# Three hand-ordered steps and 64 bytes of memory in a fused recurrence, expert and MLP kernel

## The chip, the core and the metric

The kernel runs on one core of a Trainium2 chip. The metric is the time of one execution in microseconds of the device. The engines are TensorE (PE, with its weight loads as PEld), VectorE (DVE), ScalarE (ACT), GpSimd (POOL) and SyncE (SP); SP, ACT and POOL issue transfers (SPq, ACTq, POOLq in the rows).

## The reference

Three stages follow one another. A gated linear recurrence over 768 tokens for 4 batches of 8 heads with 48 dimensions; a layer of 8 experts, in which each of the 3072 tokens goes to the expert with the largest logit; an MLP with a squared rectifier.

```
for t in range(S):                                   # attention, S = 768, D = 48
    cur = einsum('bhd,bhe->bhde', u * k[t], v[t])
    y[t] = einsum('bhd,bhde->bhe', r[t], state + cur)
    state = w[t] * state + einsum('bhd,bhe->bhde', k[t], v[t])
logits = x @ w_gate; e_idx = argmax(logits)          # x: 3072 x 384, 8 experts
out[mask] = gate * sigmoid(x @ w_output_gate)[e] * (relu(x[mask] @ w1[e]) @ w2[e])   # F = 1024
h = relu(x @ w_in); y = (h * h) @ w_out              # d_ff = 2048
```

## The kernel before

**Recurrence.** The work is cut into 16 units (4 batches times 4 pairs of heads). `load` fetches one unit's `w`, `k`, `r` and `v` in rows of 48 floats (192 bytes) into the tiles `nat` (`wN`, `kN`, `rN`, `vN`), 2 or 3 buffers of each, 128 partitions by 12 rows; a row stands every 256 bytes. These tiles are the first of the pool `ac`, which lies behind the pool `cst` of constants and small tables; a tile's address follows from the sizes of those made ahead of it. `w_check` (ACT) squares a unit's `w` for a check of its range, two units ahead; `scores` (PE) is followed by ACT copies of its banks (L738), and the turns of `k` and `r` (`k_turn`, `r_turn`, L663) reuse these banks.

**Order.** In all stages the order of instructions on each engine is the order of the code (`manual_schedule`), and each engine takes its own in that order.

**Routing.** `route_steps` of a batch makes the logits from `xT` (matmuls at L169, one per pair of heads and third of the tokens), copies them as `lt` (ACT, L172), turns them (L177), picks the expert, ranks the tokens (L216, L217) and scatters the rows to `x_rows` (POOL, L246). It is a generator: `route_step` runs it up to its next `yield`. `finish_routing` then makes the order of the experts (`bei`) and a `flag`, behind which every engine branches ("rare": values that the fast path doesn't hold for).

**Experts.** A first block of 320 tokens of expert 0 (`blkA`) starts ahead of the end of the routing, from rows of the first three batches. Its rows are gathered (`xg`, POOL, L397), scaled (DVE, L408) and turned by `prep_x` (PE, L427; hi and lo halves by ACT and DVE). `up` and `down` are its steps, nine matmuls each (L341 to L343). Behind the branch come the blocks of the 8 experts in order of size; block 0 has 128 tokens. Its words `w1r`, `w2r` are fetched in two halves by `load` (SP, L321 and L322). `expert_of` reads a number of `bei` into a register of SP. Ahead of the first words of block 1 stands a transfer of four bytes into `spare`: SP waits there for the transfers that wrote its source.

**MLP.** `down2` adds up the second product for 512 tokens in four groups of 128. In its last call the groups take the last three pieces of the hidden dimension (13, 14 and 15) one after the other; a group's end is followed by an addition (DVE, L1183) and a scatter to the output (POOL, L1185).

Of the kernel before, what the change touches and what calls it, by code (L numbers as in the profile page):

```python
# [9 lines left out]
F32 = mybir.dt.float32  # L10
F32R = mybir.dt.float32r
BF16 = mybir.dt.bfloat16
I32 = mybir.dt.int32
# [8 lines left out]
def rwkv_moe_kernel(  # L22
# [15 lines left out]
    nc = tc.nc  # L38
    B, H, S, D = r.shape
    NT, DM = out.shape  # L40
    E, _, F = w1.shape
# [26 lines left out]
    x_rows = dram.tile([NT + 1, WR], F32, name="x_rows")  # L68
# [4 lines left out]
    cst = ctx.enter_context(tc.tile_pool(name="cst", bufs=1))  # L73
# [23 lines left out]
    bvals = cst.tile([128, E, Q], F32, name="bvals")  # L97
    bcom = cst.tile([128, E], F32, name="bcom")
    bei = cst.tile([1, E], I32, name="bei")
    spare = cst.tile([1, E], I32, name="spare")  # L100
    tail = cst.tile([128, B, NTB, 2], F32, name="tail")
    xoff = cst.tile([128, E], F32, name="xoff")
    xend = cst.tile([128, E], F32, name="xend")
# [201 lines left out]
    def block_rows():  # L305
        rows_of(gi, bvals, E, B - 1)
        nc.vector.tensor_copy(off, bcom[0:1])
# [31 lines left out]
    def three(out_, a, b, a_of, b_of, start, stop):  # L339
        (ah, al), (bh, bl) = a, b  # L340
        nc.tensor.matmul(out_, a_of(ah), b_of(bh), start=start, stop=False)  # L341
        nc.tensor.matmul(out_, a_of(ah), b_of(bl), start=False, stop=False)  # L342
        nc.tensor.matmul(out_, a_of(al), b_of(bh), start=False, stop=stop)  # L343
# [204 lines left out]
    def block_of(P, k, e):  # L548
        we = [t[e:e + 1] if isinstance(e, int) else t[ds(e, 1)] for t in (w1, w2)]
        return Block(P, CAPS[k], *we, lambda n, i: gi[:n, k, i:i + 1], (k + 1) % 2)  # L550
# [7 lines left out]
    def expert_of(k):  # L558
        return nc.values_load(bei[0:1, k:k + 1], engines=(ET.SP,), min_val=0, max_val=E - 1)
# [3 lines left out]
    P = Pools("m", True)  # L563
# [6 lines left out]
    def route_step():  # L570
        return next(routing[B - 1], 0)

    with ExitStack() as actx:
# [312 lines left out]

        blkA = first["A"]
        blkA.ps_w, blkA.w_names = ps_t, ["pt"] * KD
        blkA.prep_x(0)
        blkA.prep_x(1)  # L890
        route_step()
        route_step()
        units[-1].back()
        blkA.prep_x(2)
# [9 lines left out]
    def put_ids_A():  # L904
        own = []
        for i in range(blkA.nt):
            n = blkA.rows(i)
            ins = nc.sync.dma_start(x2_ids[ds(column(offA, i) if i else 0, n)], blkA.ids[:n, i:i + 1])
            for o in own:
                tc.declare_no_dep(ins.ins, o.ins, reason="columns of their own")  # L910
            own.append(ins)

    with tc.manual_schedule(engines={ET.PE, ET.DVE, ET.Activation, ET.SP, ET.Pool}):
        put_ids_A()
        blkA.prep_w(FA, nc.vector)
        route_step()
        route_step()
        blkA.up(0)
        route_step()
        route_step()  # L920
        route_step()
        blkA.up(1)
        nc.vector.tensor_scalar(flag[:, 0:1], pf[:1, :1], 0.0, None, op0=ALU.is_le)
        blkA.down(0)
        more = None
        while more is None:
            nc.gpsimd.memset(warm, 0.0)
            more = route_step()
        tc.mark_branch_hint_location("rare", "LikelyTaken", [ET.PE, ET.DVE, ET.SP])
        finish = finish_routing()  # L930
        next(finish)
        blkA.prep_w1(FA + 1, nc.vector)
        blkA.prep_w2(FA + 1, part="hi")
        for f in range(2, FA):
            blkA.up(f)
            if f == 2:
                next(finish)
                next(finish)
                blk1 = block_of(P, 1, expert_of(1))
                nc.sync.dma_start(spare[:, 0:1].bitcast(F32), x_rows[0:1, 0:1])  # L940
                blk1.load(0)
            blkA.down(f - 1)
        for _ in finish:
            pass
        blkA.down(FA - 1)
# [4 lines left out]
    with tc.If(rare > 0, label="rare"):  # L950
        fine = nc.values_load(flag[0:1, 0:1], min_val=0, max_val=1)
        with tc.If(fine == 0):
# [57 lines left out]
                    route(b, xT, xr, fk, ps_x, True)  # L1010
            for _ in finish_routing():
                pass
            blk1.words_of(expert_of(1))
            blk1.load(0, True)
            blkA.ps_w, blkA.w_names = ps_x, ["px"] * KD
            blkA.again(FA)
            put_ids_A()
# [49 lines left out]
    NI = GT // 128  # L1067
    NPRE = 3

    FH = KF2 // 2  # L1070
# [4 lines left out]
    wi, wo, rows, ids, w2raw, converted = {}, {}, {}, {}, {}, {}  # L1075
# [69 lines left out]
    xs, gs, pos, parts = {}, {}, {}, {}  # L1145
# [17 lines left out]
    def down2(s, f, last=False):  # L1163
        fs, l = divmod(f, FH)
        if l == 0:
            pos[s] = []
            for i in range(NI):
                slot = (KD + NI * s + i) % (2 * KD)
                pos[s].append((ps_o if slot < KD else ps_x).tile([128, 512], F32, name=f"po{slot}" if slot < KD else "px"))
        for i in range(NI):  # L1170
            for q in (f - 2, f - 1, f) if last else (f,):
                three(pos[s][i][:, :DM], gs[s, q], wo[q], lambda t: t[:, i * 128:(i + 1) * 128], lambda t: t, q % FH == 0, q % FH == FH - 1)
            if l == FH - 1:
                n = s % NG * NI + i
                ob = parts.pop(n) if fs else obp.tile([128, DM], F32, name="ob")
                if fs == 0:
                    if i % 2:
                        nc.vector.tensor_copy(ob, pos[s][i][:, :DM])
                    else:
                        nc.scalar.copy(ob, pos[s][i][:, :DM])  # L1180
                    nc.sync.dma_start(part[n], ob)
                    continue
                nc.vector.tensor_tensor(ob, pos[s][i][:, :DM], ob, op=ALU.add)  # L1183
                nc.gpsimd.memset(warm, 0.0)
                ins = nc.gpsimd.indirect_dma_start(out=out[:, :], out_offset=IndirectOffsetOnAxis(ap=tokc[:, n:n + 1], axis=0),  # L1185
                                                   in_=ob, in_offset=None)
                for o in stores:
                    tc.declare_no_dep(ins.ins, o.ins, reason="rows of their own")
                stores.append(ins)
# [16 lines left out]

    with tc.manual_schedule(engines={ET.PE, ET.DVE, ET.Activation, ET.SP, ET.Pool}):
        block_rows()
        blocks = [block_of(P, 0, 0), blk1]
        blk0 = blocks[0]  # L1210
        blk0.w1t, blk0.w2t = blkA.w1t, blkA.w2t
        blk0.gather()
        atA = [column(offA, i) if i else 0 for i in range(blkA.nt)]
        blk0.banks(1)
        for f in range(FA, KF):
            blkA.up(f)
            if f + 2 < KF:
                blkA.prep_w(f + 2, nc.vector)
            if f > FA:
                blkA.down(f - 1)  # L1220
            if f == FA:
                blkA.prep_w2(FA + 1, nc.vector, part="lo")
            if f == FA + 1:
                for k in range(1, E):
                    if k == 1:
                        blk1.words_of(expert_of(k))
                    else:
                        blocks.append(block_of(P, k, expert_of(k)))
                    blocks[k].banks((k + 1) % 2)
                blocks[1].load(1)  # L1230
                convert_load(0)
            if f == KF - 1:
                blk0.prep_x(0)
# [34 lines left out]
        for n in range(KF, E * KF):  # L1268
            e, f = divmod(n, KF)
# [65 lines left out]
        for n, (s, f) in enumerate(steps2):  # L1335
            l = f % FH
# [59 lines left out]
```

## Time and profile before

| | us |
|---|---|
| median of 3 runs | 832.16 (830.5 to 833.28) |
| the profiled execution | 830.97 |
| its span, first to last instruction | 829.1 |
| PE busy in the span | 799.8 (96%) |
| DVE busy | 531.0 (64%) |
| ACT busy | 374.5 (45%) |
| POOL busy | 352.5 (43%) |

The rows further below come from the profiled execution. Times are us from the start of its span; a line such as L341 is that of the kernel. PEclk is the share of full clock that TensorE was granted (1.00 is 2.4 GHz, 0.50 is 1.2 GHz). A DMA share over 1 means that packets overlap on the transfer engines. Matmuls are pipelined, so a busy PE is not one at its peak.

### The profile page before, as it was taken

What the parts mean: (1) busy time and instruction counts of PE and PEld (TensorE: products, weight loads), DVE (VectorE), ACT (ScalarE), POOL (GpSimd) and SP (SyncE); (2) the same over time, 40 slices, a digit from 0 to 9 for tenths busy, and PEclk for the clock granted to TensorE, in tenths of its full rate; (3) what the DMA queues carried; (4) which work ended last, traced back from release to release, by engine and by line L of the source; (5) the groups of instructions that cost most, each with busy time, mean ns of one, the idle gap of its engine ahead of it and who ended that gap; (6) DMA issues with size and microseconds to landing.
All of it is one profiled execution on the core that took longest, in us unless ns stands there. A gap on an engine that the chain in (4) does not pass through costs nothing.

```text
span 829.1 us, 15685 instructions
## 1 busy us (share of the span) xinstructions
PE 799.8 (96%) x5964; PEld 724.7 (87%) x5964; DVE 531.0 (64%) x958; ACT 374.5 (45%) x792; POOL 352.5 (43%) x433
## 2 busy tenths in 40 slices
PE   4999999899999999999999999999999999999995
PEld 4888888778889999999989998888899999999994
DVE  7888899865666777788444788888533434434342
ACT  4677666633454455545453433434333333333321
POOL 7675868722534545554751333324111313212122
PEclk9999999969999999999999999999999999999998
DMA  9998899315677667678651132231203203022011
GB/s 154 156 151 128 160 149 278 109 47 193 223 121 218 194 157 281 195 194 190 200 163 57 48 124 77 96 115 58 76 18 127 92 24 114 26 90 77 1 48 38
DMA packets 157365, 102.90 MB, mean 124 GB/s; under 512 B 112350, under 2 KB 140942, under 8 KB 157286
## 3 DMA queue, kind: packets, MB, share of 16 engines
q1 hardware_dynamic: 149046, 86.55, 42.4%
q0 software_dynamic: 4912, 14.65, 5.4%
q10 hardware_dynamic: 3328, 0.66, 0.6%
q8 instruction: 48, 0.79, 0.4%
q14 instruction: 31, 0.25, 0.1%
HBM read 79.34 MB, written 22.50 MB: 123 GB/s over the span
## 4 chain that ended last, share of the span: by engine, by line
PE 60%; issue 12%; POOL 4%; DVE 0%; POOLq 0%; ACT 0%; DVEq 0%; ACTq 0%
PE ph L342 10%; PE ph L341 10%; PE ph L343 10%; PE po L341 5%; PE po L343 5%; PE po L342 5%; PE px L343 5%; PE px L341 5%; PE px L342 5%; POOL out_dram L1185 2%; PE px L427 1%; PE po L427 0%; POOL x22l L336 0%; POOL x21l L336 0%; POOL x20l L336 0%
## 5 line engine op out<-in xcount | busy, mean ns | idle before, releaser
L1160 DVE SCALAR_TENSOR_TENSOR gg<-ph,rl 128x512 f32<-128x512 f32 x96 | 66.2, 689 | 120.9 <-ACT rl L1158 120.9
L1158 ACT ACTIVATE rl<-ph 128x512 f32<-128x512 f32 x96 | 57.5, 599 | 144.6 <-PE ph L343 144.5
L336 DVE TENSOR_TENSOR gl<-gg,gh 128x512 fp32r<-128x512 f32 x96 | 66.7, 695 | 65.9 <-ACT gh L334 41.2
L334 ACT CAST gh<-gg 128x512 fp32r<-128x512 f32 x96 | 59.6, 620 | 104.3 <-DVE gg L1160 104.3
L336 POOL TENSOR_TENSOR w1l<-w1r,w1h 128x384 fp32r<-128x384 f32 x56 | 59.6, 1070 | 66.8 <-ACT w1h L334 66.4
L330 ACT ACTIVATE hh<-ph 128x320 fp32r<-128x320 f32 (+7 forms) x64 | 32.5, 508 | 114.4 <-PE ph L343 111.7
L1106 POOL TENSOR_TENSOR caf<-caf,cbf 128x384 f32<-128x384 f32 x32 | 32.6, 1018 | 114.0 <-DVE cbf L1105 114.0
L336 DVE TENSOR_TENSOR w2l<-w2r,w2h 128x384 fp32r<-128x384 f32 x64 | 64.5, 1011 | 20.1 <-ACT w2h L334 19.5
L331 DVE SCALAR_TENSOR_TENSOR hl<-ph,hh 128x320 fp32r<-128x320 f32 (+7 forms) x64 | 36.9, 576 | 38.6 <-ACT hh L330 38.3
L1185 POOL DMA_INDIRECT out_dram<-ob,tokc x24 | 23.5, 977 | 67.2 <-DVE ob L1183 65.0
L341 PE MATMUL po<-hh,w2h 128*128 128x320 f32 (+4 forms) x120 | 42.8, 357 | 0.0
L342 PE MATMUL po<-hl,w2h 128*128 128x320 f32 (+4 forms) x120 | 41.8, 348 | 0.0
L343 PE MATMUL po<-hh,w2l 128*128 128x320 f32 (+4 forms) x120 | 41.6, 347 | 0.0
L336 POOL TENSOR_TENSOR x22l<-x2r,x22h 128x512 fp32r<-128x512 f32 x12 | 15.5, 1293 | 51.5 <-ACT x22h L334 51.5
L336 POOL TENSOR_TENSOR x21l<-x2r,x21h 128x512 fp32r<-128x512 f32 x12 | 15.5, 1295 | 45.4 <-ACT x21h L334 45.4
L397 POOL DMA_INDIRECT xg<-x_rows,gi x28 | 29.1, 1039 | 11.3 <-issue 5.4
L246 POOL DMA_INDIRECT x_rows<-xr,dsi x24 | 24.1, 1005 | 22.4 <-DVE dsi L232 16.4
L334 ACT CAST w2h<-w2r 128x384 fp32r<-128x384 f32 x64 | 32.9, 516 | 0.0
L334 ACT CAST w1h<-w1r 128x384 fp32r<-128x384 f32 x64 | 32.7, 512 | 0.0
L736 PE MATMUL pt<-rA,kT 64*128 64x128 f32 x306 | 31.4, 300 | 1.0 <-DVE rA L705 1.0
L336 POOL TENSOR_TENSOR x20l<-x2r,x20h 128x512 fp32r<-128x512 f32 x12 | 15.5, 1294 | 35.9 <-ACT x20h L334 35.9
L718 POOL TENSOR_TENSOR gv<-vN,g 128x576 f32<-128x576 f32 x16 | 18.5, 1154 | 28.7 <-PE pt L663 10.7
(859 smaller groups left out, 2651.7 us busy)
## 6 DMA issues: line engine op xcount, KB each, us to landing
w1r<-in_moe_w_dram SPq DMA_DIRECT2D x16, 768.0 KB, 7.4
w2r<-in_moe_w_dram SPq DMA_DIRECT2D x16, 768.0 KB, 7.4
x2r<-x_cols SPq DMA_DIRECT2D x12, 768.0 KB, 4.9
cq<-in_moe_w_in_dram SPq DMA_DIRECT2D x16, 384.0 KB, 4.7
cq<-in_moe_w_out_dram SPq DMA_DIRECT2D x16, 384.0 KB, 6.0
vN<-in_v_dram SPq DMA_DIRECT2D x32, 144.0 KB, 4.1
part<-ob SPq DMA_DIRECT2D x24, 192.0 KB, 2.0
ob<-part SPq DMA_DIRECT2D x24, 192.0 KB, 3.1
```

Of the source, the lines that this page charges most:

```text
L330: nc.scalar.activation(hi, src, AF.Relu)
L331: nc.vector.scalar_tensor_tensor(lo, src, 0.0, hi.bitcast(F32), op0=ALU.max, op1=ALU.subtract)
L334: nc.scalar.copy(hi, src)
L336: lo_eng.tensor_tensor(lo, src, hi.bitcast(F32), op=ALU.subtract)
L341: nc.tensor.matmul(out_, a_of(ah), b_of(bh), start=start, stop=False)
L342: nc.tensor.matmul(out_, a_of(ah), b_of(bl), start=False, stop=False)
L343: nc.tensor.matmul(out_, a_of(al), b_of(bh), start=False, stop=stop)
L736: nc.tensor.matmul(pa[j][:, ci], self.kT[pp, hf * HC + ci], self.rA[pp, hf * HC + ci], start=True, stop=True)
L1106: nc.gpsimd.tensor_tensor(af, af, bf, op=ALU.add)
L1158: nc.scalar.activation(rl, ph, AF.Relu)
L1160: nc.vector.scalar_tensor_tensor(gg, ph, 0.0, rl, op0=ALU.max, op1=ALU.mult)
L1185: ins = nc.gpsimd.indirect_dma_start(out=out[:, :], out_offset=IndirectOffsetOnAxis(ap=tokc[:, n:n + 1], axis=0), in_=ob, in_offset=None)
```

## The change

It has four parts. `spare` is 24 integers long in place of 8, which moves all tiles behind it on the left side of the memory by 64 bytes. The `route_step` that holds the last logits of the last batch stands ahead of `blkA.prep_x(0)` and `prep_x(1)`. The last call of `down2` goes through its groups and pieces in a list of its own. The first words of block 1 are fetched behind the branch, after all experts' numbers were read and the rows of block 0 have landed, where the four bytes now come from; the code that fetched them again in the rare branch falls away.

```diff
-    spare = cst.tile([1, E], I32, name="spare")
+    spare = cst.tile([1, 3 * E], I32, name="spare")
...
+        route_step()
         blkA.prep_x(0)
         blkA.prep_x(1)
-        route_step()
         route_step()
         units[-1].back()
         blkA.prep_x(2)
...
             if f == 2:
                 next(finish)
                 next(finish)
-                blk1 = block_of(P, 1, expert_of(1))
-                nc.sync.dma_start(spare[:, 0:1].bitcast(F32), x_rows[0:1, 0:1])
-                blk1.load(0)
             blkA.down(f - 1)
...
-        for i in range(NI):
-            for q in (f - 2, f - 1, f) if last else (f,):
-                three(pos[s][i][:, :DM], gs[s, q], wo[q], ...)
-            if l == FH - 1:
+        order = [(i, f) for i in range(NI)]
+        if last:
+            order = [(0, f - 2), (1, f - 2), (2, f - 2), (0, f - 1), (1, f - 1), (0, f), (1, f),
+                     (2, f - 1), (2, f)] + [(NI - 1, q) for q in (f - 2, f - 1, f)]
+        for i, q in order:
+            three(pos[s][i][:, :DM], gs[s, q], wo[q], ...)
+            if q % FH == FH - 1:
...
         blk0.gather()
         atA = [column(offA, i) if i else 0 for i in range(blkA.nt)]
         blk0.banks(1)
+        for k in range(1, E):
+            blocks.append(block_of(P, k, expert_of(k)))
+            blocks[k].banks((k + 1) % 2)
+        nc.sync.dma_start(spare[:, 0:1].bitcast(F32), blk0.xg[0:1, 0, 0:1])
+        blocks[1].load(0)
...
             if f == FA + 1:
-                for k in range(1, E):
-                    if k == 1:
-                        blk1.words_of(expert_of(k))
-                    else:
-                        blocks.append(block_of(P, k, expert_of(k)))
-                    blocks[k].banks((k + 1) % 2)
                 blocks[1].load(1)
                 convert_load(0)
```

On PE, behind the recurrence's last unit (`py`), the logits are the rows with `wcat`, the turns of the first rows those with `xg`:

```order
 L169 MATMUL pt<-xT,wcat 32x256 x9
 L777 MATMUL py<-rA,St_145 64x128 x10
+L169 MATMUL pt<-xT,wcat 32x256 x3
 L427 MATMUL pt<-ident,xg 128x128 x2
 L427 MATMUL pt<-ident,xg 128x64
 L427 MATMUL pt<-ident,xg 128x128 x2
 L427 MATMUL pt<-ident,xg 128x64
-L169 MATMUL pt<-xT,wcat 32x256 x3
 L177 MATMUL pt<-ident,lt 128x96 x2
```

The three last logit matmuls stand six rows earlier, ahead of both turns; `lt`, which the last row turns, is copied from them.

On PE in the last step, `px` is the first group and `po` the others; the number behind `wo` is the piece, and `gh`, `gl` are its activations. Of the change alone, from the second group's first piece on:

```order
L341 MATMUL po_11098<-wo13h,gh 128x384
L342 MATMUL po_11098<-wo13l,gh 128x384
L343 MATMUL po_11098<-wo13h,gl 128x384
L341 MATMUL po_11099<-wo13h,gh 128x384
L342 MATMUL po_11099<-wo13l,gh 128x384
L343 MATMUL po_11099<-wo13h,gl 128x384
L341 MATMUL px<-wo14h,gh 128x384
L342 MATMUL px<-wo14l,gh 128x384
L343 MATMUL px<-wo14h,gl 128x384
```

Before, the rows of `px` with pieces 14 and 15 followed those with piece 13 at once; now two other groups' piece 13 stand between, and the second group's piece 14 stands ahead of piece 15.

On SP behind the branch (`TENSOR_LOAD` reads a register, `cq` are the conversions' loads, `x_cols` the first block's result):

```order
+L1216 DMA spare<-xg_4965 1x1
+L321 ISA
+L321 DMA w1r<-in_moe_w_dram 128x3x512
+L322 ISA
+L322 DMA w2r<-in_moe_w_dram 128x4x384
+L321 ISA
+L321 DMA w1r<-in_moe_w_dram 128x3x512
+L322 ISA
+L322 DMA w2r<-in_moe_w_dram 128x4x384
+L1078 DMA cq<-in_moe_w_in_dram 128x3x256
```

Both pairs of words now stand together there, behind nine reads of registers (two of `offA`, seven of `bei`); before, the first pair stood ahead of the branch and the second behind these nine.

## Rows read from the trace of the kernel before

**Rows 1.** Windows, three stages: length, busy us per engine (instructions), granted clock, DMA share, GB/s.

```profile
20.00:150.00 130.00, 126.65 (x2290) 112.29 (x2291) 116.18 (x233) 87.64 (x214) 91.56 (x116) 1.00 0.92 168
165.00:190.00 25.00, 21.53 (x118) 18.14 (x115) 15.15 (x68) 7.01 (x19) 6.90 (x13) 0.73 0.18 61
190.00:811.00 621.00, 620.21 (x3192) 567.90 (x3191) 366.73 (x588) 262.43 (x525) 221.89 (x225) 1.00 0.40 119
```

**Rows 2.** Windows, two stretches of input transfers, same columns.

```profile
14.00:20.00 6.00, 4.68 (x56) 4.03 (x52) 4.54 (x8) 2.83 (x6) 3.82 (x4) 1.00 1.47 166
50.00:52.00 2.00, 2.00 (x49) 1.93 (x47) 1.86 (x5) 2.00 (x5) 2.00 (x2) 1.00 0.98 187
```

**Rows 3.** Timeline of ACT and PE, 18 to 21 us: start, us, instruction [idle before, releaser].

```profile
18.55 0.78 ACT L675 ACTIVATE sq<-wN,bia 128x576 f32<-128x576 f32 x1 [3.14 <-DMA wN<-in_w_dram]
...
20.13 0.84 ACT L738 COPY A<-pt 128x384 f32<-128x384 f32 x2
...
20.69 1.24 PE L663 MATMUL pt<-ident,rN 64*128 64x64 f32 x12 [1.71 <-issue]
```

**Rows 4.** Timeline of PE, 151 to 173 us.

```profile
151.66 0.27 PE L663 MATMUL pa<-ident,rN 64*128 64x64 f32 x1 [1.43 <-DVE St L751]
...
162.44 1.50 PE L169 MATMUL pt<-xT,wcat 128*32 128x256 f32 x18
...
166.81 0.30 PE L427 MATMUL pt<-ident,xg 128*128 128x128 f32 x1 [1.54 <-DVE xg L408]
...
168.94 1.07 PE L169 MATMUL pt<-xT,wcat 128*32 128x256 f32 x6
170.49 0.58 PE L177 MATMUL pt<-ident,lt 96*128 96x96 f32 x2 [0.48 <-ACT lt L172]
...
172.75 0.64 PE L341 MATMUL ph<-x0h,w1h 128*128 128x320 f32 x1
```

**Rows 5.** Timeline of ACT and DVE, 165 to 188 us.

```profile
165.32 0.48 ACT L779 COPY xT<-py 128x384 f32<-128x384 f32 x1 [0.20 <-PE py L777]
...
185.91 0.49 DVE L331 SCALAR_TENSOR_TENSOR hl<-ph,hh 128x320 fp32r<-128x320 f32 x1 [0.22 <-ACT hh L330]
...
187.57 0.15 DVE L303 SCALAR_TENSOR_TENSOR flag<-flag 1x1 int32<-1x1 int32 x1
```

**Rows 6.** Windows, the stretch of half clock and the stretch up to the flag.

```profile
167.50:181.10 13.60, 13.05 (x60) 10.30 (x60) 8.13 (x39) 4.71 (x13) 1.21 (x3) 0.50 0.01 0
176.00:187.80 11.80, 11.80 (x67) 11.78 (x66) 9.01 (x43) 2.17 (x6) 6.43 (x12) 0.78 0.24 89
```

**Rows 7.** Timeline of SP, POOL and ACT, 192 to 210 us.

```profile
202.63 0.39 SPq L321 DMA_DIRECT2D w1r<-in_moe_w_dram  x1
...
192.13 1.04 POOL L397 DMA_INDIRECT xg<-x_rows,gi  x1 [4.94 <-DVE hl L331]
...
205.98 0.94 ACT L334 CAST w1h<-w1r 128x384 fp32r<-128x384 f32 x2
...
209.42 0.59 ACT L334 CAST hh<-px 128x512 fp32r<-128x512 f32 x1 [2.05 <-PE px L500]
```

**Rows 8.** DMA issues by tile: out<-in, engine, count, KB, median us to landing.

```profile
w1r<-in_moe_w_dram SPq DMA_DIRECT2D x16, 768.0 KB, 7.4
...
xg<-x_rows,gi POOLq DMA_INDIRECT x28, 6.2
```

**Rows 9.** Timeline of PE and POOL at the last step, 813 to 821 us.

```profile
813.88 0.44 PE L341 MATMUL px<-wo15h,gh 128*128 128x384 f32 x1 [0.87 <-ACT gh L334]
...
815.92 0.97 POOL L1185 DMA_INDIRECT out_dram<-ob,tokc  x1 [22.87 <-DVE ob L1183]
...
820.61 0.97 POOL L1185 DMA_INDIRECT out_dram<-ob,tokc  x1 [0.51 <-DVE ob L1183]
```

**Rows 10.** Timeline of POOL, the last two stores of an earlier step.

```profile
690.35 0.97 POOL L1185 DMA_INDIRECT out_dram<-ob,tokc  x1 [0.21 <-issue]
...
691.63 0.97 POOL L1185 DMA_INDIRECT out_dram<-ob,tokc  x1 [0.23 <-issue]
```

More of the change, by code (lines that the diff above doesn't have):

```diff
@@ L1012, in rwkv_moe_kernel @@
                 pass
-            blk1.words_of(expert_of(1))
-            blk1.load(0, True)
             blkA.ps_w, blkA.w_names = ps_x, ["px"] * KD
@@ L1169, in down2 @@
                 pos[s].append((ps_o if slot < KD else ps_x).tile([128, 512], F32, name=f"po{slot}" if slot < KD else "px"))
-        for i in range(NI):
-            for q in (f - 2, f - 1, f) if last else (f,):
-                three(pos[s][i][:, :DM], gs[s, q], wo[q], lambda t: t[:, i * 128:(i + 1) * 128], lambda t: t, q % FH == 0, q % FH == FH - 1)
-            if l == FH - 1:
+        order = [(i, f) for i in range(NI)]
[3 more added lines that the diff above has]
+        for i, q in order:
+            three(pos[s][i][:, :DM], gs[s, q], wo[q], lambda t: t[:, i * 128:(i + 1) * 128], lambda t: t, q % FH == 0, q % FH == FH - 1)
+            if q % FH == FH - 1:
                 n = s % NG * NI + i
@@ L1208, in rwkv_moe_kernel @@
         block_rows()
-        blocks = [block_of(P, 0, 0), blk1]
+        blocks = [block_of(P, 0, 0)]
         blk0 = blocks[0]
```

## The prediction

> **What bounds the kernel now.** I read the stages first. From 190 to 811 us TensorE (PE) is busy 620.21 of 621.00 us at full clock, and from 20 to 150 us it is busy 126.65 of 130.00 [rows 1]. In both stretches the work of PE is the time: whatever lets PE enter them sooner is kept to the end, and whatever happens to a transfer inside them costs nothing as long as PE does not wait for it. Time can be had in three places: the first 20 us, the passage from the recurrence to the experts (165 to 190 us, granted clock 0.73 in the mean), and the end. The change has a part in each, and a fourth part that moves transfers at the entry of the second stretch.
>
> The base is the profiled execution: 830.97 us, of which 829.1 are its span. The three timed runs lie at 830.5, 832.16 and 833.28; their mean with the profiled one is 831.7, 0.75 above the profiled one. I make the sum against 830.97 and add 0.75 to compare with the median.
>
> **Part 1, input tiles moved by 64 bytes.** `spare` grows from 32 to 96 bytes, so by the compiled addresses everything behind it on that side of the memory starts 64 bytes later: the pool of the input tiles goes from 90048 (448 past a multiple of 512) to 90112 (a multiple of 512). Each input row is 192 bytes, two to 512 bytes; before, each ran across a multiple of 256, afterwards none does. No instruction is added or taken away. What a faster landing could give is seen in the first 20 us: ScalarE waits 3.14 us for the third unit's `wN`, starts its check at 18.55 and can therefore copy the scores only at 20.13; PE starts its next turns at 20.69, after 1.71 us idle, when the first of these copies is done [rows 3]. So a landing that is earlier by up to 1.7 us is passed on one to one, and then into the stretch where PE is full. Would the rows land sooner? From 14 to 20 us the input moves at 166 GB/s with a DMA share of 1.47, so packets are piled up; from 50 to 52 us rows of the same size and with the same crossing move at 187 GB/s with a share of 0.98 [rows 2]. The crossing alone does not hold them at 166; but if it is what makes them pile up, 187 in place of 166 over the about 14 us up to the landing gives 14 x (1 - 166/187) = 1.6 us. If the pile comes from the source side, it gives 0. Nothing in the trace decides, so the bounds are 0 and 1.7, and I take the middle, 0.8. The other tiles that shift by 64 bytes cost nothing: their transfers lie behind the 620 us of PE.
>
> The Trainium skill, page "DMA: Bandwidth & Descriptors", section "How a descriptor splits into AXI transactions", cuts a transfer at multiples of 256 bytes and counts bytes ahead of an unaligned start as fetched too. By that rule, if it holds for the writing side, which the page does not say, a row here would take 12 beats before and 6 afterwards, and part 1 would be at its upper bound. The 187 GB/s with crossing rows [rows 2] does not show a doubling, so I do not take that bound.
>
> **Part 2, last logits ahead of the turns.** Before, PE idles 1.54 us up to 166.81 for the scaled rows, then turns them, then does the last logit matmuls (three in the code, six in the rows; 168.94, 1.07 us), then waits 0.48 us for `lt`, and only at 172.75 begins the first expert step [rows 4]. The logits need only the last copy of `xT`, which ends at 165.32 + 0.48 = 165.80 [rows 5]. At full clock 18 such matmuls took 1.50 us, so six take 0.5 [rows 4]: in the new order they run from 165.8 to 166.3, inside the hole, and cost nothing; if the hole were gone, they would cost those 0.5. The copy of `lt` then is done long before PE turns it. PE is rid of 1.07 + 0.48 = 1.55 us, and the first step begins at 171.2. But the clock is at half (0.50) from 167.5 to 181.1 [rows 6]. If that stretch stays where it is, the 1.55 us are spent on dense work at half clock, and 0.8 us is left when it ends. What sets the end of this passage is the flag on VectorE (written at 187.57), behind which all engines branch; in its last part VectorE waits 0.22 us for PE's last step [rows 5], and follows PE in all steps before it, so the flag comes 0.8 sooner, and with it the gather of the new rows. The lower bound is these 0.22; I take 0.8. The upper bound is a rival, below.
>
> **Part 3, the last step reordered.** Before, the first group of the last step needs the newest activation after six matmuls, and PE idles 0.87 us for it at 813.88, besides shorter waits. The stores go out at PE's pace, the first at 815.92, the last at 820.61 [rows 9]: three groups of nine matmuls in 4.69 us, 0.174 us each. In the new order 15 matmuls stand ahead of the first use, so PE does not wait for it. The first group still ends with the same value at the same time, so the first store stays at 815.92; the others are ready after 3, 9 and 18 more matmuls, 0.5, 1.6 and 3.1 us behind it. But GpSimd issues stores that are ready only 1.28 us apart (690.35 and 691.63) [rows 10], so they now queue there, and the last goes out at 815.92 + 3 x 1.28 = 819.8, in place of 820.61: 0.8 us won. What follows it (landing and drain, 8.5 us up to the end of the span) is taken as unchanged. Lower bound 0, if closer stores land later by as much; I take 0.8.
>
> **Part 4, words of the second block later.** Before, SP fetches them ahead of the branch; in the new order it passes the branch, reads nine registers, waits until the first gathered rows of block 0 have landed, and then issues them. The gather is issued at 192.13 [rows 7], and such gathers land after 6.2 us in the median [rows 8]: 198.3. Words land 7.4 us after issue [rows 8]: first half 205.7, second within a microsecond. ScalarE first needs them at 205.98, and it has 2.05 us free up to 209.42, the next step that PE waits for [rows 7], so until about 208 a later landing costs nothing, and beyond that it costs PE its own length. Behind the waiting DMA on SP stand the second pair of words (issued at 202.63 before, needed only after the block has begun) and the conversions' loads; they come not later than before, since SP used to read its registers only after the first pair. Nothing is gained either, since PE did not wait for the gathers. I take 0.
>
> **Sum.** 0.8 + 0.8 + 0.8 + 0 = 2.4 us: 830.97 - 2.4 = 828.6, or 829.3 beside the median. With all lower bounds the profile would be at 830.8.
>
> **Rival 1, the clock does not fall.** A hole of 1.43 us at 150.2 left the clock full; behind the hole of 1.54 and another of 0.19 us it fell [rows 4, 6]. The new order halves this hole. Without the fall PE's turns take half as long and the first step begins near 169.5, ends near 172 behind `x2l`, and the flag then is set by VectorE: 9.01 us of its own work between 176.0 and 187.8 [rows 6] from about 172.5 on, with 1 us of waits: 182.5, 5.2 us sooner than before. Then 830.97 - 5.2 - 0.8 - 0.8 = 824.2, or 824.9 beside the median. For it: the smaller hole. Against it: at half clock PE was busy 13.05 of 13.6 us and still was not raised, so more than holes counts, and the steps up to 172 stay short of dense work.
>
> **Rival 2, little comes of it.** The crossing is not what piles rows up, and the flag moves by 0.22 only, since the chain of small VectorE instructions, not PE, sets it; part 3 stays. 830.97 - 1.0 = 830.0, or 830.7 beside the median.
>
> **Rival 3, the words come too late (slower).** If SP gets through its reads no sooner than before, the first words go out where the second pair did, at 202.63 [rows 7], and land at 210.0: ScalarE, in order, holds the turned block back by 2 us over its slack. PE then idles longer than the hole behind which the clock fell, and a stretch like that of 13.6 us at 0.50 [rows 6] costs 6.8 more. 830.97 - 2.4 + 2 + 6.8 = 837.4. It decides when the words land past 208; the gather would have to land 2 us later than its median. Against it: SP no longer has its own load in flight when it branches.
>
> **Numbers.** Forecast 0.45, rival 1 0.35, rival 2 0.14, rival 3 0.06. A median differs measurably from no change here beyond 0.3%, 2.5 us. The forecast lies 2.9 below the median, so about half of its chance is faster and half is no change; rival 1 is faster, rival 2 no change. Together: faster 0.58, same 0.36, slower 0.06. The range goes from rival 1 with part 1 at its upper bound (824.0) to a little above rival 2 (831.5); the forecast alone is 827.5 to 831.
>
> **What would show it.** Part 1: ScalarE's wait at 18.55 and PE's 1.71 us shorter; equal if the crossing was harmless. Part 2: six logit matmuls ahead of 166.8, no wait for `lt`, the first step near 171 and the flag near 186.8 (rival 1: full clock through, flag near 182). Part 3: no wait for `gh` near 814, four stores 1.28 us apart. Part 4: words issued at 195 to 199, no PE wait near 206. The forecast is wrong if the half-clock stretch ends elsewhere or PE waits behind the branch.

## The result, and the profile after

Four executions of the changed kernel took 822.58 to 826.76 us, median 824.01; four of the kernel before, beside them, 830.22 to 833.28, median 831.33. The ratio is 0.9919 (95% interval 0.9898 to 0.9940): 7.3 us faster, where 2 to 3 were forecast. The profiled execution is the slowest of the four: 826.76 us with a span of 825.0, against 829.1 before. So the traces have 4.1 us to account for, and those of five points in both do it:

| stretch | before | after | gain |
|---|---|---|---|
| start to the last unit's `py` (PE, L777) | 163.87 | 160.19 | 3.68 |
| from there to PE's first step behind the branch | 25.36 | 20.93 | 4.43 |
| from there to the second block's first step | 23.40 | 28.17 | -4.77 |
| from there to the first store of the last step | 603.29 | 603.40 | -0.11 |
| first store to last store | 4.69 | 3.82 | 0.87 |

The sum is 4.10. The first line is part 1's, the second begins with part 2, the last is part 3's. The third is a loss that the forecast did not have; it stands where part 4 acts, but is not part 4's alone (below). The rows of the kernel before that these points and the readings below rest on, and that are not shown above:

```profile
13.78 0.86 ACT L738 COPY A<-pt 128x384 f32<-128x384 f32 x2 [0.37 <-PE pt L736]
...
24.99 0.48 ACT L738 COPY A<-pa 128x384 f32<-128x384 f32 x1 [3.51 <-PE pt L736]
...
28.27 1.40 PE L777 MATMUL py<-rA,St 64*64 64x128 f32 x20
...
163.87 1.40 PE L777 MATMUL py<-rA,St 64*64 64x128 f32 x20
...
186.14 0.97 POOL L246 DMA_INDIRECT x_rows<-xr,dsi  x1 [0.22 <-issue]
...
189.23 0.38 PE L341 MATMUL ph<-x0h,w1h 128*128 128x320 f32 x1 [1.18 <-PEq L950]
...
212.63 0.38 PE L341 MATMUL ph<-x0h,w1h 128*128 128x480 f32 x1
```

The windows of the changed kernel (length, busy us per engine, granted clock, DMA share, GB/s) answer to [rows 1, 2, 6]:

```profile
14.00:20.00 6.00, 5.87 (x71) 5.31 (x72) 4.52 (x8) 3.38 (x8) 4.53 (x4) 1.00 0.75 151
20.00:150.00 130.00, 125.92 (x2297) 111.58 (x2297) 118.90 (x240) 86.62 (x211) 93.68 (x122) 1.00 0.74 166
50.00:52.00 2.00, 2.00 (x52) 1.88 (x50) 1.17 (x3) 1.93 (x5) 1.71 (x3) 1.00 0.81 162
165.00:190.00 25.00, 23.13 (x152) 21.61 (x151) 17.19 (x75) 7.66 (x21) 9.42 (x15) 0.93 0.20 62
190.00:811.00 621.00, 618.04 (x3158) 566.50 (x3157) 363.82 (x575) 261.19 (x521) 218.69 (x223) 0.99 0.40 119
...
166.20:169.60 3.40, 3.40 (x12) 2.65 (x12) 1.75 (x8) 1.41 (x5) 0.00 (x0) 0.50 0.03 0
200.40:207.10 6.70, 5.85 (x24) 5.67 (x23) 2.08 (x6) 1.55 (x4) 0.21 (x1) 0.50 1.07 361
```

The share of the transfer engines from 14 to 20 us has halved, 1.47 to 0.75, and over the whole recurrence it falls from 0.92 to 0.74 at the same rate (168 and 166 GB/s): the same bytes, of all transfers there, take a fifth less of the engines' time. The half-clock stretch ahead of the branch is 3.4 us long instead of 13.6. A new one stands behind the branch, from 200.4 to 207.1 us, and PE is busy 618.04 of the 621 us from 190 on where it was busy 620.21.

Timeline of ACT and PE of the changed kernel, up to the branch (start, us, instruction [idle before, releaser]), beside [rows 3 to 5]:

```profile
12.83 0.86 ACT L738 COPY A<-pt 128x384 f32<-128x384 f32 x2 [2.13 <-PE pt L736]
...
14.31 0.81 ACT L675 ACTIVATE sq<-wN,bia 128x576 f32<-128x576 f32 x1
...
17.42 0.86 ACT L738 COPY A<-pt 128x384 f32<-128x384 f32 x2 [1.40 <-PE pt L736]
...
18.00 1.23 PE L663 MATMUL pt<-ident,rN 64*128 64x64 f32 x12
...
21.44 0.48 ACT L738 COPY A<-pa 128x384 f32<-128x384 f32 x1 [2.63 <-PE pt L736]
...
24.72 1.40 PE L777 MATMUL py<-rA,St 64*64 64x128 f32 x20
...
148.01 0.27 PE L663 MATMUL pa<-ident,rN 64*128 64x64 f32 x1 [1.43 <-DVE St L751]
...
160.19 1.40 PE L777 MATMUL py<-rA,St 64*64 64x128 f32 x20
161.52 1.28 PE L169 MATMUL pt<-xT,wcat 128*32 128x256 f32 x6
...
163.38 0.33 PE L427 MATMUL pt<-ident,xg 128*128 128x128 f32 x1 [0.25 <-DVE xg L408]
...
164.75 0.38 PE L177 MATMUL pt<-ident,lt 96*128 96x96 f32 x2
...
166.93 0.63 PE L341 MATMUL ph<-x0h,w1h 128*128 128x320 f32 x1
...
181.12 0.39 PE L341 MATMUL ph<-x0h,w1h 128*128 128x320 f32 x1 [1.31 <-DVEq L947]
```

The check of `wN` at 14.31 no longer waits for a transfer (18.55 with 3.14 us of wait before), the copies at 17.42 and the turns of `rN` at 18.00 come 2.7 us sooner, and PE's 1.71 us of idle ahead of these turns are gone. At the first `py` the lead is 3.55 us (28.27 before), at the hole near 150 it is 3.65: the whole gain of part 1 is made in the first 28 us and then kept. Behind the last `py` the six logit matmuls stand where PE idled 1.54 us; the waits for scaled rows shrink to a quarter of a microsecond, the one for `lt` is gone.

Timeline of the flag and of what follows it, engine by engine, beside [rows 5] and [rows 7]:

```profile
179.48 0.15 DVE L303 SCALAR_TENSOR_TENSOR flag<-flag 1x1 int32<-1x1 int32 x1
...
180.57 0.97 POOL L246 DMA_INDIRECT x_rows<-xr,dsi  x1 [0.23 <-issue]
...
186.62 0.99 POOL L397 DMA_INDIRECT xg<-x_rows,gi  x1 [5.00 <-DVE w2l L336]
...
191.70 0.93 POOL L397 DMA_INDIRECT xg<-x_rows,gi  x1 [0.30 <-issue]
...
190.78 0.44 SPq L321 DMA_DIRECT2D w1r<-in_moe_w_dram  x1
...
192.74 0.80 SPq L322 DMA_DIRECT2D w2r<-in_moe_w_dram  x1
...
196.01 0.42 DVE L408 TENSOR_SCALAR xg<-xg 128x384 f32<-128x384 f32 x1 [1.48 <-DMA xg<-x_rows,gi]
198.80 0.95 DVE L408 TENSOR_SCALAR xg<-xg 96x384 f32<-96x384 f32 x1 [2.37 <-DMA xg<-x_rows,gi]
...
199.80 0.30 PE L427 MATMUL po<-ident,xg 96*128 96x96 f32 x1 [2.10 <-DVE xg L408]
...
201.34 0.69 PE L343 MATMUL px<-w2h,hl 128*128 128x384 f32 x1 [0.85 <-DVE hl L336]
...
209.29 0.38 PE L341 MATMUL ph<-x0h,w1h 128*128 128x480 f32 x1
```

GpSimd issues the gathers of the first and second block from 186.62 to 191.70, and from 190.78 on SP issues all four transfers of words, 3 MB, into the same queues. The last gathered rows land only near 198.8; VectorE waits 1.48 and 2.37 us for them, PE 2.10 us behind it and then 0.85 us for what VectorE does next, and in these waits the clock falls. The flag (179.48) and GpSimd's last scatter ahead of these gathers (180.57) are taken up under part 4.

Timeline of the last step, beside [rows 9]:

```profile
810.99 0.33 PE L341 MATMUL px<-wo15h,gh 128*128 128x384 f32 x1
...
812.69 0.97 POOL L1183 DMA_INDIRECT out_dram<-ob,tokc  x1 [22.89 <-DVE ob L1181]
...
813.97 0.97 POOL L1183 DMA_INDIRECT out_dram<-ob,tokc  x1 [0.21 <-issue]
...
816.51 0.97 POOL L1183 DMA_INDIRECT out_dram<-ob,tokc  x1 [0.22 <-issue]
```

PE takes the first `wo15` without a wait, and the stores stand 1.28 us apart. From the last store to the end of the span it is 8.49 us, as before.

### The profile page after: what moved, and what is told of

Its sections match the earlier page's. It is cut to its first block, busy times and chain, and to the rows that moved or that the text cites. A ratio compares the mean times of both kernels' runs of the same rounds, so it can differ in the third digit from the quotient of the medians.

```text
span 825.0 us, 15674 instructions
## 1 busy us (share of the span) xinstructions
PE 797.5 (97%) x5964; PEld 724.4 (88%) x5964; DVE 530.5 (64%) x958; ACT 374.2 (45%) x792; POOL 352.0 (43%) x433
## 4 chain that ended last, share of the span: by engine, by line
PE 69%; issue 13%; DVE 8%; POOL 5%; DMA 3%; ACT 1%; POOLq 0%; DVEq 0%; SPq 0%; ACTq 0%
PE ph L341 9%; PE ph L342 9%; PE ph L343 9%; PE po L341 5%; PE px L343 5%; PE px L341 5%; PE po L343 5%; PE po L342 5%; PE px L342 5%; POOL out_dram L1183 2%; PE pt L736 2%; PE py L767 2%; PE pt L663 1%; DVE suf L684 1%; PE py L777 1%
## 5 line engine op out<-in xcount | busy, mean ns | idle before, releaser
L336 POOL TENSOR_TENSOR x22l<-x2r,x22h 128x512 fp32r<-128x512 f32 x12 | 15.5, 1294 | 51.5 <-ACT x22h L334 51.5
L336 POOL TENSOR_TENSOR x21l<-x2r,x21h 128x512 fp32r<-128x512 f32 x12 | 15.5, 1294 | 45.5 <-ACT x21h L334 45.5
L336 POOL TENSOR_TENSOR x20l<-x2r,x20h 128x512 fp32r<-128x512 f32 x12 | 15.5, 1291 | 36.0 <-ACT x20h L334 36.0
```

Of the source, the lines that this page charges most:

```text
L336: lo_eng.tensor_tensor(lo, src, hi.bitcast(F32), op=ALU.subtract)
```

## The experiments

All were timed in turn with the kernel before on their own chip. On the chips of e5 to e7 and of e12 the kernel before took 835.05 and 834.14 us, on the others 831.2 to 831.5; so ratios are compared, and times only within one group.

### Part 1: what do 64 bytes do?

**e1_align** makes part 1 alone, the longer `spare`.

> Part 1 alone (`spare` of 24 integers, all else as before). Theory: the shift of the input tiles is worth what the traces of before and after differ by up to the end of the recurrence (PE's turn behind `St` of the last unit at 151.66 before, 148.01 after: 3.6 us), because rows that run across a multiple of 256 bytes land more slowly. Then this kernel is about 3.6 us faster than before (827.7 beside 831.3), the DMA share from 14 to 20 us falls from 1.47 to under 1, and the rest of the program, routing and half-clock stretch included, is that of before, only sooner. Rival: the recurrence was sooner in that one execution by chance or because of the other parts; then the time moves by 0.8 us or less.

Measured: 826.92 us against 831.21, ratio 0.9953 (0.9936 to 0.9970), 4.3 us faster. Windows of e1_align:

```profile
14.00:20.00 6.00, 5.63 (x74) 5.12 (x74) 4.63 (x8) 3.66 (x8) 4.53 (x4) 1.00 0.98 196
20.00:150.00 130.00, 126.00 (x2281) 112.17 (x2279) 117.39 (x236) 86.60 (x210) 93.13 (x121) 0.99 0.74 165
```

The theory's 3.6 us hold for the start: the first `py` is at 24.45, 3.82 us sooner. In this profile 1 us of it is lost between 120 and 150 us, where the clock fell (granted 0.94). How the median comes to 4.3 one profile does not show.

**e8_gap128** and **e9_gap32** leave `spare` as it was and put an unused tile of 128 or 32 bytes at the head of the input pool, so that only the tiles of that pool and of the working pool behind it move. Rows of 192 bytes then start 64 or 224 past a multiple of 256; before, 192.

```diff
+        ac.tile([128, 32], F32, name="gap")        # e9_gap32: [128, 8]
         nat = {(nm, i): ac.tile([128, NC, 2, 64], F32, ...
```

> The kernel before with an unused tile of 128 bytes at the head of the input pool: the input rows of 192 bytes start 64 past a multiple of 256 (before: 192 past it), so none runs across a multiple of 256, but none starts at one either; the constants and tables stay where they were. Theory (the crossing costs): as fast as part 1 alone, 3.5 to 4.3 us under before, DMA share from 14 to 20 us under 1. Rival (the start has to be a multiple of 256 or 512): no gain. Second rival (the other shifted tiles made the gain of part 1): no gain either.

> The kernel before with an unused tile of 32 bytes at the head of the input pool: the rows start 224 past a multiple of 256 and still run across it. Theory (the crossing costs): the time of before within 1 us, DMA share from 14 to 20 us above 1.2. Rival (any shift changes which rows share something else): a gain or loss of 2 us or more.

Measured: e8_gap128 826.89 us against 831.49, ratio 0.9945 (0.9925 to 0.9965); e9_gap32 831.98 us, ratio 0.9996 (0.9984 to 1.0009). Windows of e8_gap128, in which no row crosses:

```profile
14.00:20.00 6.00, 5.70 (x70) 5.07 (x68) 4.52 (x8) 3.59 (x8) 4.52 (x4) 1.00 0.90 178
20.00:150.00 130.00, 125.90 (x2293) 111.67 (x2294) 118.81 (x237) 86.68 (x210) 93.64 (x121) 1.00 0.74 166
```

and of e9_gap32, in which every row crosses:

```profile
14.00:20.00 6.00, 4.73 (x58) 4.08 (x54) 4.54 (x8) 2.85 (x6) 3.77 (x4) 1.00 1.40 164
20.00:150.00 130.00, 126.73 (x2254) 112.92 (x2256) 113.48 (x226) 85.61 (x210) 90.74 (x115) 0.99 0.93 168
```

Its ScalarE waits as before:

```profile
18.57 0.78 ACT L676 ACTIVATE sq<-wN,bia 128x576 f32<-128x576 f32 x1 [3.12 <-DMA wN<-in_w_dram]
```

So it is where the rows are written, and neither the start at a multiple (64 past it does as well) nor the tables that part 1 moves too. The sources of the rows are the same in all four kernels.

All profiles agree. The first `py` begins at 28.27 to 29.38 us in the four kernels whose rows cross (before, e2_logits, e3_words, e9_gap32) and at 24.45 to 25.60 in the ten others. The traces record each packet: of the 98304 packets of 192 bytes, 39 to 42% take longer than 15 ns where rows cross, 20.2 to 20.6 ns in the mean (22.3 to 22.9 in the first 20 us); where they do not, 1.4 to 1.6% do, and the mean is 15.5. One thing is not separated: every second of the rows that cross also crosses a multiple of 512, and only some of the packets take longer.

### Part 2: the logits and the clock

**e2_logits** makes part 2 alone, the move of one `route_step`.

> Part 2 alone (the last logits ahead of the turns of the first rows). Theory: it shortens the stretch of half clock from 13.7 to about 3.4 us and brings the flag 4 to 5 us sooner, as between the traces of before and after (25.36 us from the last `py` to the first step behind the branch, 20.93 after). The words of the second block stay ahead of the branch here, so nothing is given back: about 4 us faster (827). Rival: the short half-clock stretch of after needs part 1 or part 4 as well; alone the stretch stays at 13 us and only 0.2 to 0.8 us are won (830.5 to 831.1).

Measured: 828.62 us against 831.21, ratio 0.9965 (0.9952 to 0.9979), 2.6 us faster: between the two. The window from the last `py` to the first step behind the branch, in e2_logits:

```profile
164.21:187.90 23.69, 21.56 (x130) 18.45 (x128) 14.79 (x64) 7.17 (x19) 7.69 (x14) 0.78 0.21 69
```

The table has, for each profile, the times from the last `py` to three points, and the mean granted clock up to the first. What the mean clock lacks, twice over, is the share at half clock: 25.36 x 2 x (1 - 0.73) = 13.7 us before.

| kernel | part 2 | to PE's first step behind the branch | clock | to the first gather behind it | to the second block |
|---|---|---|---|---|---|
| before, e3_words | no | 25.36, 25.45 | 0.73, 0.73 | 28.26, 28.38 | 48.76, 48.80 |
| e8_gap128 | no | 24.49 | 0.79 | 27.35 | 48.02 |
| e1_align, e9_gap32 | no | 22.60, 22.82 | 0.85, 0.85 | 28.05, 28.17 | 48.20, 48.43 |
| e2_logits | yes | 23.69 | 0.78 | 26.59 | 47.37 |
| e4_no_words | yes | 22.24 | 0.85 | 25.17 | 46.01 |
| after, e10_no_words | yes | 20.93, 20.77 | 0.92, 0.92 | 26.43, 26.10 | 49.10, 46.33 |
| e11_after | yes | 19.01 | 1.00 | 24.44 | 46.86 |

(The profiles of e5 to e7 and e12 are left out: PE is held at the branch there, or ScalarE ahead of it.)

Up to the branch, at the same clock, the new order is worth 0.4 us (22.24 for 22.60) to 0.8 us (23.69 for 24.49). The rest is how long the clock stays low, and that differs from execution to execution in both orders. From 0.73 to 0.85 the old order loses 6.9 us of half clock and 2.76 us of length, 0.40 us each. But little of this lasts: at the second block e1_align and e9_gap32 are only 0.3 to 0.6 us ahead of before and e3_words. What lasts is in the last two columns. With part 2 the first gather goes out 24.4 to 26.6 us behind the last `py`, without it 27.4 to 28.4, and where part 4 is not beside it the second block begins after 46.0 to 47.4 us, in place of 48.0 to 48.8 (48.02 to 48.76 without e3_words), 1.8 us less in the mean.

Over all runs the mean granted clock was 0.9934 for e2_logits (12 runs) and 0.9894 for the kernel before (23): 829 x 2 x 0.0040 = 6.6 us less at half clock. At 0.40 each that would be the whole 2.6 us measured. But among the 23 runs of the kernel before, a run with 0.001 more clock, 1.66 us less at half clock, is only 0.28 us shorter (a straight line through widely scattered runs): 0.17 each, 1.1 us in all. So the clock alone does not make the 2.6.

### Part 4: words and rows

**e3_words** makes part 4 alone, **e4_no_words** parts 1 to 3 without it.

> Part 4 alone (first words of the second block fetched behind the branch). Theory: the gathered rows of the second block now share the queues with 3 MB of words, PE waits for them near 207 us and falls to half clock there for some 7 us: 3 to 5 us slower than before (834 to 836). Rival, as forecast: it costs nothing (831.3), because here the flag is as late as before and all scatters are done by then; the loss in after would then come from the early flag.

> Parts 1 to 3 without part 4. Theory: the 4.8 us that after loses behind the branch (23.40 us from the branch to the first step of the second block before, 28.17 after) are part 4's, and come back: about 4 to 5 us faster than after (819.5 to 820.5; 831.3 - 3.6 - 4.4 - 0.9 = 822.4 if all three parts are worth what the traces show and no more), PE at full clock behind 171 us and no wait near 200. Rival: with the flag this early, the words fetched ahead of the branch hold up SP and the gathers as well, PE waits there too, and the time stays at that of after (824) within 1 us.

Measured: e3_words 832.38 us against 831.21, ratio 1.0021 (1.0009 to 1.0034), 1.2 us slower. In its profile, the fastest of its executions, the last tile of rows does come late, but PE does not wait for it:

```profile
204.65 0.42 DVE L408 TENSOR_SCALAR xg<-xg 96x384 f32<-96x384 f32 x1 [1.66 <-DMA xg<-x_rows,gi]
...
206.24 0.44 PE L341 MATMUL px<-w2h,hh 128*128 128x384 f32 x1 [0.31 <-ACT hh L334]
```

e4_no_words 824.35 us, ratio 0.9924 (0.9907 to 0.9940). That is the changed kernel's own time: the 4 to 5 us that I expected back did not come. In its profile the entry is clean (23.77 us from the branch to the second block, no wait for rows), its whole span 822.5. So 4.4 us do come back there, but 1.9 are lost again ahead of the branch; and the changed kernel's execution that I compared with was its slowest, 826.76, where the other three took 822.6 to 824.3.

**e10_no_words** is e4_no_words and **e11_after** the changed kernel, in turn on one chip.

> Parts 1 to 3 without part 4 again, beside the changed kernel on the same chip and in turn with it. If part 4 costs what one profile of the changed kernel shows in every execution, this one is 3 to 5 us faster; if that wait comes only in some executions, 0 to 1.5 us faster in the median; part 4 alone cost 1.2 us against before.

> The changed kernel beside the one above. Expected from both profiles so far: 0.9925 to 0.994 of before. In its profile: input DMA share under 1 from 14 to 20 us, the last logits ahead of the turns, four stores 1.28 us apart; open is whether PE waits for gathered rows near 200, as in one of two profiles.

Measured: 824.64 us, ratio 0.9907 (0.9890 to 0.9924), and 826.27 us, ratio 0.9931 (0.9908 to 0.9953). Leaving part 4 out is 1.6 us faster here, though the intervals overlap. Timeline of e11_after:

```profile
199.18 1.18 DVE L408 TENSOR_SCALAR xg<-xg 96x384 f32<-96x384 f32 x1 [2.64 <-DMA xg<-x_rows,gi]
...
200.41 0.30 PE L427 MATMUL po<-ident,xg 96*128 96x96 f32 x1 [2.11 <-DVE xg L408]
```

and of e10_no_words:

```profile
193.57 0.33 PE L427 MATMUL px<-ident,xg 128*128 128x128 f32 x1 [1.58 <-DMA xg<-x_rows,gi]
```

PE waits in both, for the second block's rows with part 4 and for the first block's without it, and in e4_no_words, the same program as e10_no_words, it does not wait. What differs is how late the rows are asked for. GpSimd begins the gathers 4.1 to 5.1 us after it has done with the last of its six scatters to `x_rows`, in every profile but that of e7_rows_first (8.2 us), whenever the flag comes. From before to after, the flag (187.57, 179.48) and PE's first step come 8.1 us sooner, the last scatter (186.14, 180.57) and the first gather (192.13, 186.62) only 5.6 and 5.5. So in the changed kernel the gathers stand 5.5 us behind PE's first step, before 2.9. The profiles of chips without the hold fall into four cells, us from PE's first step to the second block:

| first gather behind PE's first step | without part 4 | with part 4 |
|---|---|---|
| 2.9 us | 23.40, 23.53, 23.68, 23.77 (before, e8, e2, e4) | 23.35 (e3) |
| 5.3 to 5.5 us | 25.56, 25.60, 25.61 (e10, e1, e9) | 27.85, 28.17 (e11, after) |

Late gathers cost 1.8 to 2.2 us by themselves (PE waits 1.5 to 1.6 us for the first block's rows), words beside late gathers another 2.2 to 2.6, and words beside early ones nothing: in e3_words the last rows are as slow as in after, 7.2 and 7.1 us from their issue (3.0 before), but PE does not need them yet. So of the 4.77 us lost in the first profile, about 2 come with the early flag and the rest with part 4. e9_gap32 shows late gathers without any part of the change, behind a short half-clock stretch. The cells are read from one profile of each kernel; no experiment moved the scatters alone. They would also explain the 1.2 us of e3_words: of its twelve runs six took 830.9 to 831.7 us and six 833.1 to 835.0, but only the first kind was profiled.

The clock fell behind the waits of the changed kernel (granted 0.94 from 181 to 212 us in e11_after) and not behind that of e10_no_words (1.00).

**e5_after** is the changed kernel with a second profile; **e6_hold** holds the second pair of words back until the second block's rows have landed; **e7_rows_first** holds all words back.

e6_hold:

```diff
         blocks[1].load(0)
+        blocks[1].gather()
         for f in range(FA, KF):
...
+                nc.sync.dma_start(spare[:, 1:2].bitcast(F32), blocks[1].xg[0:1, NTL - 1, 0:1])
                 blocks[1].load(1)
...
-        blocks[1].gather()
         blkA.down(KF - 1)
```

e7_rows_first:

```diff
-        nc.sync.dma_start(spare[:, 0:1].bitcast(F32), blk0.xg[0:1, 0, 0:1])
+        blocks[1].gather()
+        nc.sync.dma_start(spare[:, 0:1].bitcast(F32), blocks[1].xg[0:1, NTL - 1, 0:1])
         blocks[1].load(0)
...
-        blocks[1].gather()
         blkA.down(KF - 1)
```

> The changed kernel once more, timed side by side with the two that follow, and with a second profile. If the loss of 4.8 us behind the branch that its first profile shows is part of every execution, the second profile shows it too: the scaled rows of the second block wait for gathered rows, PE waits about 2 us near 200 and falls to half clock. If it is an accident of that one execution (826.76, the slowest of four), the second profile has no such wait and lies at 822 to 824.

> The changed kernel, but the second pair of words is issued only when the last gathered rows of the second block have landed (four more bytes into `spare`, and the gathers written ahead of them in the code). Theory: rows and 3 MB of words collide; with 1.5 MB less beside them the rows land by 196 instead of 198.7, PE has no wait near 200 and keeps its clock: 23.5 us from the branch to the second block's first step, as before, and 821 to 822 in the median, 2 to 3 faster than the changed kernel. Rival: the first pair alone delays the rows as much, or the second pair then comes too late for the second block: no gain, 824 or more.

> The changed kernel with all words behind the rows: the four bytes that the first words wait for come from the last gathered tile of the second block instead of the first block's. If the words are the collision, no row waits and `xg` is scaled without a DMA wait; the words then go out near 195 and land near 199.5, within what ScalarE has free: 821 to 822. If words that come late are the danger (rival 3 of the prediction), ScalarE waits for `w1r` near 198 to 201 and PE behind it: 825 or more.

Measured, against 835.05: e5_after 828.92 us, ratio 0.9943 (0.9921 to 0.9965); e6_hold 830.39, 0.9952 (0.9933 to 0.9970); e7_rows_first 829.83, 0.9940 (0.9918 to 0.9962). Neither hold is measurably faster than the changed kernel. Timeline of e5_after:

```profile
185.68 0.38 PE L341 MATMUL ph<-x0h,w1h 128*128 128x320 f32 x1 [3.26 <-DVE twk L273]
...
202.29 0.42 DVE L408 TENSOR_SCALAR xg<-xg 96x384 f32<-96x384 f32 x1 [1.08 <-DMA xg<-x_rows,gi]
```

On this chip PE stands 3.26 us at the branch (1.31 in the first profile), VectorE and GpSimd do not, so the rows have 2 us more before PE asks for them (the gathers stand 3.5 us behind its first step): the last of them is 1.08 us late for VectorE, and PE does not wait near 200. A gain from moving the words could hardly show here. In e6_hold the hold made a wait of its own: VectorE scales the rows in place and must let the four bytes be read first.

```profile
205.09 0.42 DVE L408 TENSOR_SCALAR xg<-xg 96x384 f32<-96x384 f32 x1 [3.10 <-DMA spare<-xg]
```

**e12_rows_first** is e7_rows_first on another chip.

> The changed kernel with all words behind the second block's rows, once more, on another chip. In its first profile no instruction waited for gathered rows and none for words, and from the branch to the second block's first step it took 24.4 us (27.9 and 28.2 in the two profiles of the changed kernel in which rows and words collided); but that chip was slower for every kernel, and ScalarE stood still there for 5 us ahead of the branch. If the collision is what part 4 costs, the ratio to before is 0.989 to 0.991, that of parts 1 to 3 without part 4 or a little better (823 to 824), with about 23.5 us from the branch to the second block. If the late words cost as much as the collision, the ratio is that of the changed kernel, 0.992 to 0.993 or more.

Measured: 830.47 us against 834.14, ratio 0.9951 (0.9932 to 0.9970). The gain did not come. Its profile has no wait of VectorE or PE for gathered rows behind the branch and none for words, but this chip too holds PE at the branch:

```profile
186.63 0.61 PE L341 MATMUL ph<-x0h,w1h 128*128 128x320 f32 x1 [3.35 <-DVE twk L273]
```

So whether words behind the rows are worth anything stays open: in both profiles the gathers are nearer to PE's first step than the 5.5 us of the changed kernel. In e12_rows_first they stand 3.5 us behind it, and 2.7 in e7_rows_first, where ScalarE stands idle for 8.22 us up to 186.20 and the flag is late.

## Why the prediction was right, and where it was not

The direction was right, and the range held the time by a hundredth of a microsecond: 824.01 against its lower end of 824.0. That end was rival 1 with part 1 at its upper bound, and that it met the time is luck. The forecast itself (829.3 beside the median) was not: in the traces the gains are 9.0 us (3.68, 4.43 and 0.87) in place of 2.4, and 4.8 us are lost that were not in the sum.

**Part 1, mis-sized: 0.8 forecast, bounds 0 to 1.7; measured 3.55 in the traces, 4.3 and 4.6 in the times of e1_align and e8_gap128.** The mechanism (crossing) was named, and two steps went wrong. The first is "a landing that is earlier by up to 1.7 us is passed on": 1.7 was PE's one idle stretch ahead of the turns, but the copies ahead of it were late as well and so was the next unit. The three pairs of copies come 0.95, 2.71 and 3.55 us sooner (13.78, 20.13, 24.99 before; 12.83, 17.42, 21.44 after): the stretch that I named gives 1.76, and 0.95 ahead of it and 0.84 behind it were missed. The second is the inference from 50 to 52 us that "the crossing alone does not hold them at 166". Later rows had time; that a rate is reached there says nothing of what a row costs. The time of the packets says it: 20.2 ns with crossing and 15.5 without, 1.30 times as much, and 22.3 for 15.0, 1.49 times, in the first 20 us (before and after). Over all transfers of the recurrence, most of which are such rows, it is 1.23 times: 0.92 of the engines for 168 GB/s, 0.74 for 166.

The Trainium skill, page "DMA: Bandwidth & Descriptors", section "How a descriptor splits into AXI transactions", speaks of bytes that are read. If its rule holds for the side that is written, a crossing row would by an estimate from it be twice as dear (12 beats for 6), and a row that starts 64 past a multiple of 256 would pay for the bytes ahead of it. The sign here is that of the rule. The size is not, 1.30 to 1.49 times instead of 2, and rows from 64 on cost no more than rows from 0 on: 15.5 ns and a share of 0.74 in both. I was wrong to let the one rate at 50 us speak against the upper bound.

**Part 2, the clock and the gathers, not the flag.** At equal clock the 0.8 forecast stands at the upper end of the 0.4 to 0.8 measured up to the branch. Two steps failed. "If that stretch stays where it is": in the first profile the clock fell for 3.4 us in place of 13.6, and over the runs of e2_logits there were 6.6 us less at half clock in the mean. Rival 1 (the clock does not fall) was the nearer case; in e11_after the clock was full from the last `py` to the branch, having fallen ahead of it (granted 0.87 from 148.87 us to the last `py`). Why the stretch is short in one execution and long in the next, in both orders, the runs do not tell. The second step is "so the flag comes 0.8 sooner, and with it the gather": from the last `py` the flag came 4.4 us sooner (23.70, 19.29) and the gather 1.8 (28.26, 26.43), since GpSimd's scatters set it. So rival 1 has the gain to the branch about right and is silent on what is given back behind it. Two readings were slightly off: the 0.22 us are in their row a wait for ScalarE's `hh`, one step behind PE, and rival 1's 5.2 us are 5.1 by its own terms (187.57 - 182.5).

**Part 3, right.** 0.8 forecast, 0.87 measured in the trace, by the way described: no wait for `gh`, four stores at 1.28 us, an unchanged tail. It was not run alone; but in all eight profiles with it the stores take 3.82 or 3.83 us from first to last, in all six without it 4.69.

**Part 4, wrong: 0 forecast, 1.2 us of loss alone, and 2.2 to 2.6 us in the profiles where the gathers are late.** The step that failed is "PE did not wait for the gathers", taken from a trace in which the gathers were early and had the queues to themselves after the first words. I asked when words have to be there, found them in time (they were, and sooner than forecast: issued 4.2 us behind the first gather, at 190.78, not 6.2), and did not ask what else would be in the queues by then, nor whether part 2 would bring the gathers forward as far as PE. Rival 3 had the right chain (a wait of PE longer than the hole, then a fall of the clock) on the wrong transfer: rows, not words.

The parts measured alone, -4.3, -2.6 and +1.2 us, with -0.87 for part 3 from the trace, sum to -6.6, between the changed kernel's 7.3 faster in the first comparison and 5.2 in e11_after. Whether the change is better without part 4 is not settled: 0.9907 and 0.9924 of before without it, 0.9919, 0.9931 and 0.9943 with it (the last on a slower chip), and 1.6 us faster without it in the one comparison on the same chip.

## What to carry to other kernels

Look at where short rows stand in the memory before looking at their number: rows of 192 bytes that cross a multiple of 256 cost 1.3 times the packet time here, and two shifts that keep them inside one, by 64 and by 128 bytes, cured it alike. Size such a gain over the whole start, not over one idle stretch, since every early step that waits for a landing moves with it. When a step is moved earlier, ask of each engine behind it whether it moves too: here the flag and PE did, and GpSimd's scatters, and the gathers behind them, moved less. List also what else will be in the transfer queues at the new time. A wait of 2 us on TensorE cost the clock as well in two profiles.

## What the runs showed of the hardware

Transfers into rows that cross a multiple of 256 bytes: 20.2 to 20.6 ns for a packet of 192 bytes in the mean, DMA share 0.92 and 0.93 at 168 GB/s. Rows that do not cross, from 0 or from 64: 15.5 ns, and 0.74 at 165 and 166 GB/s. The length of a half-clock stretch at one and the same place varies between executions of nearly the same program, from a granted clock of 0.73 to 1.00 over some 20 to 25 us. The last of five gathers of rows landed 3.0 us after its issue in the kernel before, and 7.1 us after it in the changed kernel, with 3 MB of loads beside it. Chips differ: on the two where the kernel before took 834 to 835 us, e5_after and e12_rows_first hold PE for 3.3 us at the branch instead of 1.3, and take 16.0 and 17.0 us instead of 12.2 from the hole near 150 to the last `py`.
